# A chunked delta-rule recurrence with a channel mix: inputs w and a in a tile apart from b and k with earlier loads, a readout in four array pieces and two banks, and a mix in 768-column instructions

## The chip, the cores and the metric

One core of one Trainium2 chip runs the whole kernel. The metric is the device time of one execution, in microseconds (us); lower is better.

## The reference

Six arrays r, k, v, w, a, b of shape 4 batches x 8 heads x 768 steps x 40 go through a recurrence over the steps with a 40x40 state per head; what it reads out goes through a channel mix with three weight matrices.

```python
for t in range(S):
    y[:, :, t] = einsum('bhd,bhde->bhe', r[t], state)
    Sa = einsum('bhde,bhe->bhd', state, a[t])
    state = state * w[t][:, :, None, :] - outer(Sa, b[t]) + outer(v[t], k[t])
x = y as (batch, step, 320); x_prev = x one step earlier
xk = mu_k * x + (1 - mu_k) * x_prev;  xr likewise with mu_r
out = sigmoid(xr @ w_r) * (relu(xk @ w_k) ** 2 @ w_v)      # 320x320, 320x1024, 1024x320
```

All is float32. The two inputs of a matrix product of the channel mix are split into a high and a low part, and three partial products are added.

## The kernel before

**Tiling.** The 768 steps are cut into 12 chunks `k` of 64 (`C`). The 32 heads are handled in two parts `p` of 16; within a part two heads are stacked on the partitions (rows 0 to 39 and 64 to 103, `ROWS`; `EP` = 104) and eight such pairs lie side by side (`G` = 8). Inside a chunk the recurrence is turned into small matrix products and one triangular solve.

**The steps of a chunk.** `front` (four pieces on the vector engine, DVE: a running product of w, a reverse scan, w times a into `az`, and the decay times b and k) and the scores `psc` and transposes `pkt` run two chunks ahead of the chunk that uses them. Before a front, `check` has the scalar engine (ACT) test that w lies in range; it reads the first part of the loaded tile. The triangular solve `tri` is a recurrence of 30 steps on GpSimd (POOL), two chunks ahead as well: `tri_out` writes the 32x32 blocks of the scores to DRAM, `tri` reads them back in another layout and solves, `tri_store` writes the result to DRAM, `tri_back` reads it into `sn`. The chain of the chunk itself has five stages, z, T, L, U, s: 64 small matmuls each (lines 413, 419, 425, 431, 437), and after each a copy on ACT (`zs`, `vu`) that the next stage needs. T and the stages behind it read the solved `sn`. Then come `put`, `pgh`, the readout `py` (lines 499 and 504) and the product with the decay on DVE (`xp`). `send_x` moves `xp` by DMA into `x` in the layout of the channel mix; `Mix` does the channel mix of that chunk during the next two chunks, one piece at a time.

**What sets the order.** Everything is recorded in the order in which it is written (`manual_schedule`), and each engine works its own instructions off in that order, DMA issues on the queue of SyncE (SP) included. `STEP` is a hand-written list of 25 slots, numbered 0 to 24, that every chunk goes through; a word is a step and its part (`w0`: load for part 0). `M` is one piece of Mix (or, at first, of the conversion of the weights), `F` one piece of a front. `later(n, ...)` puts an instruction off to the end of the n-th slot from here.

```python
STEP = [x.split() for x in (
    "z0 z1 F", "M F r0", "T0 T1 F", "M pmt0 q1 r1", "L0 L1 F", "M pmt1 F", "U0 U1 F", "M psc0 F", "s0 s1", "M psc1", "M put0 to",
    "M put1 v", "M pgh0", "M tl", "py0", "M pgh1 ts", "M pkt0", "M py1", "pkt1 tk", "M w0 x", "M w1", "M", "M",
    "M Q0", "M F")]
AHEAD = dict(r=(0, load_rv), w=(3, load_wab), Q=(3, check), q=(2, check), psc=(2, scores), pkt=(2, pkt))
```

So `w0` in slot 19 of chunk k loads all of w, a, b and k of chunk k+3, part 0, as one tile `wab`, and `Q0` in slot 23 has ACT read it. `wab` has two buffers; the one that is filled was read last by `pkt0` in slot 16. `w1` and `q1` (slot 3 of the next chunk) are the same for part 1. Before slot 0 of chunk 0 a prologue loads and prepares chunks 0, 1 and part of 2.

**Banks.** The tag `sw` has three PSUM banks, taken in turn by `psc` (2 each), `put` (2), `pgh` (2), `py` (1), `pkt` (2) and `pmt` (1): whoever takes one waits until what was written there three takes earlier has been read out.

## Time and profile before

| what | value |
|---|---|
| times of three runs | 703.68, 711.09, 702.17 us |
| the profiled execution: span from its first to its last instruction | 707.3 us |
| its own time | not given beside the span; the span lies among the three times |
| busy: PE, DVE, ACT, POOL | 541.4, 440.4, 313.9, 396.5 us |
| mean granted TensorE clock | 0.843 |
| moved by DMA | 71.15 MB, mean 101 GB/s |
| stages by the starts of line 413: prologue; chunk 0; 1; 2; 3 to 9 together; 10; 11 and the rest | 76.8; 56.7; 82.8; 44.1; 343.4; 33.9; 69.6 us |

PE is the matmul engine, PEld its weight loads. "Lnnn" is a line of the kernel. In the timeline a row is: start, duration, engine, line, operation, out<-in, count, and in brackets the idle time ahead of it and what ended that. In the views of waits a row is: who waited, for whom, total us, how often, the longest.

### The profile page before, as it was taken

What the parts mean: (1) busy time and instruction counts of PE and PEld (TensorE: products, weight loads), DVE (VectorE), ACT (ScalarE), POOL (GpSimd) and SP (SyncE); (2) the same over time, 40 slices, a digit from 0 to 9 for tenths busy, and PEclk for the clock granted to TensorE, in tenths of its full rate; (3) what the DMA queues carried; (4) which work ended last, traced back from release to release, by engine and by line L of the source; (5) the groups of instructions that cost most, each with busy time, mean ns of one, the idle gap of its engine ahead of it and who ended that gap; (6) DMA issues with size and microseconds to landing.
All of it is one profiled execution on the core that took longest, in us unless ns stands there. A gap on an engine that the chain in (4) does not pass through costs nothing. (4 is left out here: it accounts for less than half of the span.)

```text
span 707.3 us, 24797 instructions
## 1 busy us (share of the span) xinstructions
PE 541.4 (77%) x10658; PEld 496.2 (70%) x10658; DVE 440.4 (62%) x773; ACT 313.9 (44%) x793; POOL 396.5 (56%) x814
## 2 busy tenths in 40 slices
PE   1103256605498999989989979899799799999994
PEld 1103245505398888979878979889798799999984
DVE  6577558629846828738648468287386476463551
ACT  2112142114346546445545445464455445656562
POOL 4286683860078369388388585792882883830000
PEclk9999996555578895895988968958959859999998
DMA  5532757482245264463583563644635706332100
GB/s 139 115 92 43 181 111 136 118 189 62 48 100 132 68 131 105 102 128 70 115 159 67 115 140 70 130 103 102 128 71 114 167 21 128 86 79 67 45 25 23
DMA packets 120555, 71.15 MB, mean 101 GB/s; under 512 B 96574, under 2 KB 110870, under 8 KB 118150
## 3 DMA queue, kind: packets, MB, share of 16 engines
q1 hardware_dynamic: 118214, 63.74, 42.6%
q10 hardware_dynamic: 2223, 5.76, 3.1%
q8 instruction: 85, 1.39, 0.8%
q14 instruction: 33, 0.26, 0.1%
HBM read 52.98 MB, written 10.22 MB: 89 GB/s over the span
## 5 line engine op out<-in xcount | busy, mean ns | idle before, releaser
L387 POOL TENSOR_TENSOR td<-td,ttmp 128x30 f32<-128x30 f32 (+4 forms) x360 | 175.3, 487 | 28.2
L384 POOL TENSOR_TENSOR ttmp<-ta,td 128x30 f32<-128x30 f32 (+4 forms) x360 | 174.1, 484 | 28.3
L112 PE MATMUL ph<-xk,wkh 120*128 120x256 f32 x480 | 99.6, 306 | 6.2 <-ACT xk L90 5.2
L378 POOL TENSOR_SCALAR_AFFINE_SELECT td<-ta 64x512 f32<-64x512 f32 x24 | 18.4, 765 | 139.2 <-DMA ta<-tx 138.1
L90 DVE TENSOR_TENSOR hl<-hf,hh 128x256 fp32r<-128x256 f32 x96 | 43.2, 450 | 64.4 <-ACT hh L90 63.7
L112 PEld LDWEIGHTS ph<-xk,wkh 120*128 120x128 f32 x480 | 75.5, 200 | 10.8 <-ACT xk L90 5.7
L333 PE MATMUL psc<-az,wab 40*64 40x64 f32 x1536 | 39.4, 275 | 54.0 <-DVE wab L318 43.2
L333 PEld LDWEIGHTS psc<-az,wab 40*64 40x64 f32 x1536 | 35.6, 184 | 58.8 <-issue 55.7
L306 DVE TENSOR_TENSOR_SCAN pe<-wab,first 104x520 f32<-104x520 f32 x24 | 31.1, 1296 | 67.5 <-ACT pe L90 46.7
L90 ACT ACTIVATE hf<-ph 128x256 f32<-128x256 f32 x96 | 36.6, 381 | 75.8 <-PE ph L112 75.5
L112 PE MATMUL pv<-wvh,hh 128*128 128x320 f32 x192 | 68.8, 358 | 1.8 <-issue 1.8
L419 PE MATMUL ch<-zs,sn 32*32 32x40 f32 x768 | 21.9, 229 | 62.6 <-ACT zs L90 62.6
L112 PE MATMUL ph<-xk,wkl 120*128 120x256 f32 x288 | 68.2, 292 | 0.0
L419 PEld LDWEIGHTS ch<-zs,sn 32*32 32x32 f32 x768 | 20.1, 134 | 65.3 <-ACT zs L90 64.7
L112 PE MATMUL pv<-wvh,hl 128*128 128x320 f32 x192 | 61.6, 321 | 0.0
L112 PE MATMUL pv<-wvl,hh 128*128 128x320 f32 x192 | 61.3, 319 | 0.0
L90 POOL TENSOR_TENSOR mc<-zs,pe 104x320 f32<-104x320 f32 x24 | 17.9, 767 | 58.7 <-DVE zs L90 58.0
L112 PEld LDWEIGHTS ph<-xk,wkl 120*128 120x128 f32 x288 | 50.7, 201 | 0.0
L90 DVE TENSOR_TENSOR az<-psc,mask 64x512 f32<-64x512 f32 x48 | 33.1, 689 | 22.3 <-PE psc L333 21.5
L90 ACT COPY vu<-ch 32x320 f32<-32x320 f32 x96 | 40.0, 416 | 12.9 <-PE ch L419 11.3
L112 PEld LDWEIGHTS pv<-wvh,hh 128*128 128x128 f32 x192 | 37.7, 197 | 6.0 <-issue 2.1
L90 ACT ACTIVATE hf<-hf 128x256 f32<-128x256 f32 x96 | 40.0, 417 | 3.1
(95 smaller groups left out, 1213.2 us busy)
## 6 DMA issues: line engine op xcount, KB each, us to landing
wab<-in_wab_dram SPq DMA_DIRECT2D x22, 835.7 KB
vr<-in_rvd_dram SPq DMA_DIRECT2D x24, 416.0 KB
ta<-tx SPq DMA_DIRECT2D x24, 256.0 KB
vu<-in_vt_dram SPq DMA_DIRECT2D x24, 256.0 KB
out_dram<-sig SPq DMA_DIRECT2D x48, 80.0 KB
tx<-sn SPq DMA_DIRECT2D x48, 64.0 KB
ty<-td SPq DMA_DIRECT2D x24, 128.0 KB
sn<-ty SPq DMA_DIRECT2D x48, 64.0 KB
```

The costliest lines, as they stand in the source:

```text
L90: f(*args, **kw)
L112: nc.tensor.matmul(out, lhsT=left[i][g], rhs=right[j][g], start=start and k == 0, stop=stop and k == len(terms) - 1)
L306: nc.vector.tensor_tensor_scan(out=pe.rearrange("p x t -> p (x t)"), data0=w[:, 0:SP], data1=first, initial=0.0, op0=ALU.mult, op1=ALU.add)
L333: nc.tensor.matmul(to[64 * y:64 * y + 64, x], lhsT=kb[r0:r1, x, y], rhs=az[r0:r1, i, x], start=True, stop=True)
L378: nc.gpsimd.affine_select(out=TD[h], in_=TA[h, i::2], compare_op=ALU.is_gt, fill=0.0, base=-i, pattern=[[-2, 16], [1, 32]], channel_multip ...
L384: nc.gpsimd.tensor_tensor(out=tmp, in0=TA[:, s:s + 1, s + 1:].broadcast_to([128, rows, n]), in1=TD[:, 0:rows, s:s + 1].broadcast_to([128, ...
L387: nc.gpsimd.tensor_tensor(out=TD[:, 0:rows, s + 1:], in0=TD[:, 0:rows, s + 1:], in1=tmp, op=ALU.subtract)
L419: mm(c3[a:a + 32, x], lhsT=sn[a:a + 32, x, 0:32], rhs=zs[a:a + 32, x], start=True, stop=True)
```

## The change

The input `wab` becomes two: `wa` (w and a, 104x1033) and `kb` (b and k, 104x1024), each in tiles of its own with two buffers. `wa` of chunk k+3 is loaded in slots 3 and 8 of chunk k, `kb` in slots 18 and 20. In the readout the state's transposed copy `mk` is one dense 104x104 block per pair, not four padded ones, so that the first half of `py` runs on 40-row pieces, and the two heads of a pair go to two banks, each with its own `xp`. In the mix, the difference, the high and the low part are one instruction of 768 columns each in place of three of 256, and the mix has five pieces in place of seven. In the start-up the order of the constants on POOL changes, and mu_k and mu_r are loaded behind the first inputs and weights.

```diff
-    "z0 z1 F", "M F r0", "T0 T1 F", "M pmt0 q1 r1", "L0 L1 F", "M pmt1 F", "U0 U1 F", "M psc0 F", "s0 s1", "M psc1", "M put0 to",
-    "M put1 v", "M pgh0", "M tl", "py0", "M pgh1 ts", "M pkt0", "M py1", "pkt1 tk", "M w0 x", "M w1", "M", "M",
+    "z0 z1 F", "M F r0", "T0 T1 F", "M pmt0 q1 r1 a0", "L0 L1 F", "M pmt1 F", "U0 U1 F", "M psc0 F", "s0 s1 a1", "M psc1",
+    "M put0 to", "M put1 v", "M pgh0", "M tl", "py0", "M pgh1 ts", "M pkt0", "M py1", "pkt1 tk b0", "M x", "M b1", "M", "M",
     "M Q0", "M F")]
...
-                for g in range(3):
-                    nc.vector.tensor_tensor(out=d4[:, g], in0=x[:, g, :, 1:], in1=x[:, g, :, 0:C], op=ALU.subtract)
+                nc.vector.tensor_tensor(out=diff.rearrange("p g b t -> p (g b) t", b=NB),
+                                        in0=by_b[:, :, 1:], in1=by_b[:, :, 0:C], op=ALU.subtract)
                 yield
...
-                    for g in (2, 0, 1):
-                        xm = moe.tile([128, TT4], F32, tag="xm", name="xm", bufs=2)[:NP] if nm == "k" else diff[:, g]
+                    xm = moe.tile([NP, 3, TT4], F32, name="xm") if nm == "k" else diff
+                    for g in range(3):
                         nc.vector.scalar_tensor_tensor(
...
-                        later(0, nc.scalar.copy, hi[:, g], xm)
-                        later(1, nc.vector.tensor_tensor, out=lo[:, g], in0=xm, in1=hi[:, g].bitcast(F32), op=ALU.subtract)
-                        if g == 2:
-                            later(2, nc.sync.dma_start, lo[80:120, 2].bitcast(F32), hi[40:80, 2].bitcast(F32))
-                        yield
+                        if g == 1:
+                            yield
+                    later(0, nc.scalar.copy, hi, xm)
+                    later(1, nc.vector.tensor_tensor, out=lo, in0=xm, in1=hi.bitcast(F32), op=ALU.subtract)
+                    later(2, nc.sync.dma_start, lo[80:120, 2].bitcast(F32), hi[40:80, 2].bitcast(F32))
+                    yield
...
-            def load_wab(k, p, parts=((0, WP + 3 * G * C),)):
+            def load_wa(k, p, parts=((0, WP + G * C),)):
+                x = att.tile([EP, WP + G * C], F32, tag="wa", name=f"wa_{k}_{p}", bufs=2)
...
+            def load_kb(k, p):
+                x = st[k, p]["kb"] = att.tile([EP, G, 2, C], F32, tag="kb", name=f"kb_{k}_{p}", bufs=2)
+                nc.sync.dma_start(x, kb[k, p])
...
-                for q, (r0, r1) in enumerate(ROWS):
-                    later(0, nc.scalar.copy, mk[r0:r1, :, :, q, 0:HD], p4[r0:r1, :, :, 0:HD])
+                later(0, nc.scalar.copy, mk, pt[0:EP].rearrange("d (x e) -> d x e", x=4)[:, :, 0:EP])
...
-                y = ps("sw", f"py_{k}_{p}").rearrange("e (x t) -> e x t", t=C)
+                ys = [ps("sw", f"py_{k}_{p}_{q}").rearrange("e (x t) -> e x t", t=C) for q in range(2)]
...
-                            nc.tensor.matmul(y[r0:r0 + n, 2 * x + q], lhsT=mk[:, x, i, q, 0:n], rhs=r[:, x, i],
+                            nc.tensor.matmul(ys[q][r0:r0 + n, x], lhsT=mk[d0:d1, x, r0:r0 + n], rhs=r[d0:d1, x, i],
...
-                for x in range(4):
-                    for q in range(2):
+                for q in range(2):
+                    for x in range(4):
...
+                for q in range(2):
+                    later(0, nc.vector.tensor_tensor, out=xp[:, q], in0=ys[q][0:EP, 0:4].rearrange("e (b j) t -> e b j t", b=2),
...
-            AHEAD = dict(r=(0, load_rv), w=(3, load_wab), Q=(3, check), q=(2, check), psc=(2, scores), pkt=(2, pkt))
+            AHEAD = dict(r=(0, load_rv), a=(3, load_wa), b=(3, load_kb), Q=(3, check), q=(2, check), psc=(2, scores), pkt=(2, pkt))
```

On SP's queue, from `tk` (the read-back into `sn`, slot 18) of one chunk to the scores' way out (`tx<-sn`, slot 10) of the next, this stands before (x is the channel mix's input, vr the tile of v and r):

```order
L371 DMA sn_4004<-ty 32x16x32 x4
L277 DMA wab_0_5360<-in_wab_dram 104x2057
L521 DMA x_5362<-xp_5187 40x12x64 x2
L523 DMA x_5362<-xp_5187 40x4x64 x3
L277 DMA wab_1_5381<-in_wab_dram 104x2057
L400 DMA vr_0_5484<-in_rvd_dram 104x4x256
L400 DMA vr_1_5544<-in_rvd_dram 104x4x256
L90 DMA xk<-xk 40x256
L362 DMA tx<-sn_5660 32x16x32 x4
```

And this of the changed kernel at the same place:

```order
L377 DMA sn_3174<-ty 32x16x32 x4
L284 DMA kb_0_4515<-in_kb_dram 104x1024
L526 DMA x_4526<-xp_4351 40x12x64 x2
L528 DMA x_4526<-xp_4351 40x4x64 x3
L284 DMA kb_1_4545<-in_kb_dram 104x1024
L406 DMA vr_0_4646<-in_rvd_dram 104x4x256
L406 DMA vr_1_4707<-in_rvd_dram 104x4x256
L279 DMA wa_0_4709<-in_wa_dram 104x1033
L85 DMA xk<-xk 40x256
L279 DMA wa_1_4890<-in_wa_dram 104x1033
L368 DMA tx<-sn_4818 32x16x32 x4
```

The half with w and a, which `check` reads, has moved behind vr and is now that of the chunk after: it is issued a chunk earlier relative to its use. The half with b and k stands where `wab` stood.

On DVE, from the `hl` of slot 13 (the low part of the mix's hidden layer) to the masked scores of `pgh1` in slot 15 (`gh_1`), this stands before:

```order
L90 TENSOR_TENSOR hl<-hf,hh 128x256
L90 TENSOR_TENSOR xr<-diff,xr 120x256
L90 TENSOR_TENSOR hl<-hf,hh 128x256
L90 TENSOR_TENSOR xr<-diff,xr 120x256
L90 TENSOR_TENSOR xp_6843<-py_0_6810,pe_0_4586 104x2x4x64
L147 SCALAR_TENSOR_TENSOR diff<-diff,mur,x_6190 120x256
L90 TENSOR_TENSOR gh_1_0_6861<-pgh_1_0_6863,mask 128x512
L90 TENSOR_TENSOR gh_1_1_6862<-pgh_1_1_6864,mask 128x512
```

And this of the changed kernel:

```order
L85 TENSOR_TENSOR hl<-hf,hh 128x256 x2
L85 TENSOR_TENSOR xr<-diff,xr 120x768
L85 TENSOR_TENSOR xp_6817<-py_0_0_6783,pe_0_4578 104x2x2x64
L85 TENSOR_TENSOR xp_6817<-py_0_1_6784,pe_0_4578 104x2x2x64
L85 TENSOR_TENSOR gh_1_0_6834<-pgh_1_0_6836,mask 128x512
L85 TENSOR_TENSOR gh_1_1_6835<-pgh_1_1_6837,mask 128x512
```

All of the low part of xr now stands ahead of `xp`, in one instruction, and `xp` is two instructions, one for each bank; `pgh1` takes the bank that the first of them frees.

## The prediction

> **What bounds the kernel now.** The page comes first: its slices show where the span goes.

> ```profile
> PE   1103256605498999989989979899799799999994
> PEclk9999996555578895895988968958959859999998
> ```

> From slice 12 on PE is busy nearly all the time, yet the granted clock falls to about half once in every chunk. A busy PE is then a slow PE. So the stages come next, cut at the starts of the chain (line 413); the columns are start:end and length, the busy us of PE, PEld, DVE, ACT and POOL, the granted clock, DMA's share and GB/s:

> ```profile
> 216.30:260.40 44.10, 42.26 (x891) 38.55 (x890) 30.89 (x54) 25.25 (x64) 26.57 (x51) 0.88 0.47 104
> 260.40:310.10 49.70, 46.66 (x889) 42.92 (x888) 31.23 (x54) 24.52 (x63) 33.25 (x67) 0.79 0.52 104
> ...
> 553.50:603.80 50.30, 46.65 (x890) 42.87 (x889) 31.89 (x57) 24.48 (x63) 34.00 (x69) 0.80 0.48 104
> 603.80:637.70 33.90, 33.90 (x729) 31.44 (x728) 18.90 (x38) 20.15 (x53) 18.91 (x46) 1.00 0.36 82
> 216.30:637.70 421.40, 394.31 (x7833) 361.55 (x7832) 269.57 (x465) 216.78 (x558) 279.06 (x558) 0.84 0.50 105
> ```

> Chunks 3 to 9 take 49.1 us each (603.8 - 260.4, by 7) at a clock of 0.79 to 0.89. Chunk 10, which has no chunk 12 to prepare, takes 33.9 at 1.00. One of the slow chunks, number 6, cut in three:

> ```profile
> 405.40:412.50 7.10, 3.14 (x73) 2.83 (x72) 1.46 (x3) 2.31 (x7) 6.08 (x13) 1.00 0.86 172
> 412.50:430.60 18.10, 18.06 (x351) 16.62 (x351) 15.81 (x23) 10.07 (x25) 16.32 (x23) 0.53 0.40 88
> 430.60:454.60 24.00, 24.00 (x472) 21.95 (x470) 14.14 (x29) 12.10 (x32) 11.86 (x33) 1.00 0.56 114
> ```

> PE stands still for 4 us early on, then works for 18.1 us at 0.53, then at full clock. Who stops it, by the waits of PE, ACT and POOL over chunks 3 to 9 (who, for whom: us, times, longest), and the timeline at that place:

> ```profile
> PE ch L419 <- ACT zs L90: 24.0, 7, 4.0
> ACT pe L90 <- DMA wab<-in_wab_dram: 28.2, 6, 5.2
> POOL td L378 <- DMA ta<-tx: 74.8, 12, 11.7
> 402.78 0.40 SPq L277 DMA_DIRECT2D wab<-in_wab_dram  x1
> 410.13 0.72 ACT L90 ACTIVATE pe<-wab,limit 104x512 f32<-104x512 f32 x1 [5.20 <-DMA wab<-in_wab_dram]
> 412.00 0.74 ACT L90 COPY zs<-ch 128x320 f32<-128x320 f32 x2
> 412.48 1.60 PE L419 MATMUL ch<-zs,sn 32*32 32x40 f32 x64 [3.96 <-ACT zs L90]
> ```

> The 836 KB load is issued at 402.78 and lands some 7 us later. ACT works in order: `check` (pe) waits for the load, and `zs`, which stage T needs, stands behind it. All seven chunks show it: 24.0 us, 3.4 each. The lost clock costs more: at 0.53, 18.1 us do the work of 9.6, 8.5 us lost.

> **The change, part by part.** *The load of w and a* now goes out in slots 3 and 8 for a use in slot 23 and in slot 3 of the next chunk, more than 20 us ahead where 7 sufficed for twice the bytes. Its buffer is free once the front two chunks ahead has run, before it is issued; what queues behind it on SP (xk, the scores' way out) needs the same fronts anyway. So ACT's wait goes: 3.4 us, and the half-clock stretch behind it with it. b and k arrive for slots 2 and 7, nine slots after slot 18: hidden, while SP isn't late.

> *The readout.* Line 499 runs 32 instructions on whole rows; `pgh` (line 483) already has the 40-row pieces that it will have:

> ```profile
> 439.28 1.15 PE L499 MATMUL py<-vr,mk 104*64 104x64 f32 x32
> 440.21 1.11 PE L504 MATMUL py<-gh,kt 128*40 128x64 f32 x32
> 442.39 1.16 PE L483 MATMUL pgh<-vr 40*64 40x64 f32 x64
> 443.48 0.42 PE L112 MATMUL pv<-wvh,hh 128*128 128x320 f32 x1
> ```

> From start to start 32 take 0.93 us, and pgh's 64 take 1.09; 32 such take 0.55. Two readouts a chunk save 0.8 us of PE.

> *The mix and the second bank.* Widths that exist give the price of 768 columns:

> ```profile
> L139 DVE TENSOR_TENSOR diff<-x 120x256 f32<-120x256 f32 x36 | 19.1, 580 | 0.0
> L90 DVE TENSOR_TENSOR gh<-pgh,mask 128x512 f32<-128x512 f32 x48 | 30.9, 685 | 15.3 <-PE pgh L483 15.3
> L318 DVE TENSOR_TENSOR wab<-wab 104x1024 f32<-104x1024 f32 x24 | 31.5, 1312 | 0.4
> L90 ACT CAST xr<-diff 120x256 fp32r<-120x256 f32 x36 | 14.5, 402 | 1.2 <-DVE diff L147 1.2
> L90 ACT COPY sn<-psc 128x512 f32<-128x512 f32 x24 | 14.1, 586 | 39.0 <-PE psc L333 39.0
> ```

> On DVE 768 lies half-way between 685 and 1312 ns, 1.0 us; on ACT 402 and 586 ns continue to 0.77. A chunk's `diff` goes from 1.74 to 1.0 us, each low part from about 1.4 to 1.0, and the two halves of `xp` cost 0.27 more per part: about 1 us less of DVE's 31 per chunk. ACT saves about 1.6 of 24.5 (mixes 0.9, `mk` in one copy 0.7). Neither bounds a chunk, so I count nothing. But `pgh1` now takes a bank that the first `xp` must empty, and all of xr's low part stands ahead of `xp`:

> ```profile
> 440.25 0.41 ACT L90 CAST hh<-hf 128x256 fp32r<-128x256 f32 x1
> ```

> Chunk 6: hh ends at 440.66, xr's high part at 441.4, its low part at 442.4, the first `xp` (about 0.5, 256 columns) at 442.9; pgh1, due at 442.39 - 0.4 = 442.0, would wait 0.9 us. Its bounds are 0 (DVE gets there earlier) and 1.8 (as much again, with ACT and DVE late by one instruction each); I take 0.9. Behind it on PE stands all the rest of the chunk.

> *The fronts on DVE.* In the first two stretches of chunk 6 DVE is busy for 1.5 + 15.8 = 17.3 us, where PE without stall and throttle needs 3.1 + 9.6 = 12.7. The fronts must end before the second scores, due at about 14 (12.7 and one more piece of mix, 1.3). Of the 17.3, some 2 isn't front and stands behind, and the mix saves 0.5 here: 14.8, so a wait of 0.8. Its bounds are 0 (fronts that start ahead of slot 0) and 17.3 - 12.7 = 4.6; I take 1.0.

> *PE's floor.* Without stall and throttle chunk 6 takes 3.1 + 9.6 + 24.0 = 36.7 us; less 0.8, plus 0.9 and 1.0: **37.8**.

> *What is late next: POOL.* The solve, the two `mc` behind it, the wait, and the last solve, beside which no front runs:

> ```profile
> 433.60:435.10 1.50, 1.50 (x16) 1.24 (x16) 1.46 (x3) 0.71 (x3) 1.43 (x2) 1.00 0.23 34
> 435.10:444.40 9.30, 9.30 (x234) 8.37 (x232) 7.92 (x18) 5.29 (x15) 0.00 (x0) 1.00 0.76 178
> 444.40:481.60 37.20, 34.00 (x576) 31.69 (x574) 21.64 (x34) 17.62 (x45) 31.85 (x64) 0.73 0.49 97
> 593.60:624.20 30.60, 30.60 (x632) 28.16 (x632) 14.59 (x30) 18.88 (x50) 25.00 (x64) 1.00 0.39 86
> 433.18 0.59 ACT L90 COPY sn<-psc 128x512 f32<-128x512 f32 x1 [0.71 <-PE psc L333]
> 442.80 1.28 SPq L367 DMA_DIRECT2D ty<-td  x2
> 448.38 2.90 SPq L371 DMA_DIRECT2D sn<-ty  x4
> ```

> POOL needs 37.2 + 1.5 = 38.7 us a chunk and idles 9.3, most of which a 37.8 us chunk no longer has. The DVE work that lay in these 9.3 us (7.9 busy) then lies beside a solve. The bounds: it stretches nothing (38.7), or each of its microseconds blocks POOL (46.6). The two solves are nearest: 7.0 us more of DVE cost 6.6, but that was the fronts, which ran beside the solve already. For the rest I take 1.3: POOL's pace is **40.0 us**.

> When that bites: the scores leave PE at 433.2, 27.8 into chunk 6 and 15.3 without stall and throttle; `ta` lands 11.2 later, the solve takes 37, the way back into `sn` 8.5 (442.80 to 451.28) and a landing of about 2 (an estimate): 74 us into a chunk, where T two chunks on comes at 2 x 37.8 + 3 = 78.6. A lead of 4.6, lost at 2.2 a chunk (and 0.9 less at the first): chunks 2 to 6 go at PE's floor, 7 to 9 at 40.0, and chunk 10, which waits for the last solve, takes some 37. What PE then waits for is `sn` at T and, since x stands behind `tk` on SP, a late x on DVE.

> [...]

> *The start-up.* Two small loads no longer stand ahead of the first one, and `check` of chunk 2 waits for half the bytes:

> ```profile
> 0.83 0.48 SPq L102 DMA_DIRECT2D muk<-in_mu_k_dram  x1
> 1.36 0.34 SPq L102 DMA_DIRECT2D mur<-in_mu_r_dram  x1
> 95.70 0.72 ACT L90 ACTIVATE pe<-wab,limit 104x512 f32<-104x512 f32 x1 [7.18 <-DMA wab<-in_wab_dram]
> 159.10 2.34 PE L419 MATMUL ch<-zs,sn 32*32 32x40 f32 x64 [23.53 <-ACT zs L90]
> ```

> 0.8 for the first, 2 for the second (bounds 0 and 3.6, half of the wait). In chunk 1 ACT keeps T waiting for 23.5 us, behind weight loads among which the chunk-3 inputs come too; half of these now go earlier: 3 us (bounds -2 and 10). Together 6.

> *The sum*, for the profiled execution: 5 x 37.8 + 3 x 40.0 + 37 = 346 us, where the row says 421.4: 75.4 less. With the start-up 81.4. The last 69.6 us (PE-bound from the start of chunk 11) stay. 707.3 - 81.4 = 625.9; the profiled execution lies 3.6 us above the median of 703.7, so **622 us** for the median.

> **The rivals.** *The clock stays low.* Chunk 2 had no wait at T, and yet:

> ```profile
> 225.95 0.63 PE L112 MATMUL pv<-wvh,hh 128*128 128x320 f32 x1 [1.84 <-issue]
> ```

> After 1.84 us of standstill the clock was halved and the chunk took 44.1. If each of the smaller waits left (0.9 at pgh1, 1.0 at the scores, up to 2 for `sn`) does this, chunks take 44.1 - 0.8 = 43.3: 8 of them and chunk 10 with 34 make 380, 41 less; with the start-up **657**. Against it: a halved chunk is slower than POOL, which then regains its lead, so that the next ones don't wait; the mean falls back to POOL's pace. [...]

> *POOL keeps up* (its lower bound or better): 8 x 37.8 + 34 = 336, 85 less; with the start-up **613**. It needs a solve near 35 us; those beside fronts took 37.

> *DVE blocks POOL fully*, the upper bound of POOL's pace: 2 x 37.8 + 6 x 46.6 + 37 = 392, 29 less: **668**. For it the two solves, against it the 14.6 us of DVE beside the last, unstretched one.

> *The change doesn't do what it says*, since DMA is the limit: then b and k come late at slot 2 and DVE, then PE, waits as long as now. For it: the 7 us landing, and 0.86 DMA share at 172 GB/s ahead of the stall. Against it: a mean share near 0.5. Only the start-up and the readout are left, 6 and 8 x 0.8: **691**.

> *Slower: the second bank.* If pgh1's wait reaches the 1.84 us of chunk 2, the clock is halved in the dense second half as well; 17 us at half cost 8.5. With a first halving in place (43.3) and the longer wait a chunk takes 43.3 + 1.8 + 8.5 = 53.6, 4.5 more than now: 8 x 4.5 - 6: **734**. It decides at a wait of some 1.8 us, twice what I find.

> **How the numbers follow.** Forecast 0.50 (own range 612 to 642), clock 0.25, POOL keeps up 0.11, DVE blocks POOL 0.04, wait not removed 0.06, second bank 0.04. The range goes from 604, where POOL keeps up and the two new waits are half of what I took, to 664, which leaves out the last three and a part of the clock's case. A measurement of this kernel tells 2% from no change: below 689.6 is faster. The first four are, 0.90; the wait not removed is mostly within 2%, 0.06; slower 0.04.

> **What the new profile would show.** ACT's wait of `pe` for a DMA gone from chunk 2 on; no 3 us gap ahead of line 419's stage, or one whose `sn` is late; POOL without its 9 us wait for `ta`, solves of 37 to 39 us end to end; chunks of 38, then 40 us; a clock near 1.0 in the chunks; a gap below 1 us at pgh1, released by `xp`. Wrong I would be if the clock is halved again in each chunk, if POOL still idles while PE waits, or if DVE waits for b and k.

## The result, and the profile after

The changed kernel takes 634.5 us (median of four runs, 627.5 to 636.4) where the kernel before takes 703.5 in the same rounds: a ratio of 0.902, 95% interval 0.895 to 0.908. The forecast was 622 with a range of 604 to 664: the sign and the main mechanism were right, the size was 12 us too good. The profiled execution has a span of 634.4 us.

The page's slices of TensorE's busy share and of its granted clock, after the change:

```profile
PE   2204238534569999999899999999999899999995
PEclk9999998555558789999999999999999999999999
```

The clock no longer falls once per chunk: from slice 15 on (238 us) it stays at nine tenths or more. The same by stages, cut at the starts of stage z (chunks 2, 3, 6, 9, 10, and 11 with the rest; the columns are as in the prediction):

```profile
206.10:249.90 43.80, 42.19 (x889) 38.17 (x888) 30.48 (x50) 24.28 (x59) 26.41 (x49) 0.88 0.49 112
249.90:289.70 39.80, 38.04 (x889) 34.38 (x888) 31.23 (x50) 22.98 (x58) 34.97 (x66) 1.00 0.59 134
370.00:410.40 40.40, 38.23 (x891) 34.39 (x890) 31.63 (x50) 23.07 (x58) 35.49 (x67) 1.00 0.57 133
490.30:531.50 41.20, 38.22 (x889) 34.43 (x888) 32.00 (x52) 22.54 (x57) 36.14 (x69) 1.00 0.47 103
531.50:565.90 34.40, 33.83 (x729) 30.95 (x728) 17.96 (x34) 19.06 (x47) 20.76 (x47) 1.00 0.38 82
565.90:634.40 68.50, 58.84 (x907) 54.76 (x906) 27.70 (x58) 34.22 (x83) 1.44 (x2) 0.98 0.16 37
```

Chunks 3 to 9 take 281.6 us, 40.2 each, where they took 343.4, 49.1 each: 62 of the 73 us that the span lost. All seven stand at clock 1.00 in this execution. The start-up (to the start of chunk 2) went from 216.3 to 206.1. Chunk 2 alone is still halved and takes 43.8. What TensorE waits for in chunks 3 to 9 now:

```profile
PE py L503 <- DVE gh L85: 3.9, 7, 0.6
PE ch L443 <- ACT vu L85: 3.3, 5, 1.0
PE ch L437 <- issue: 2.3, 3, 0.9
PE psc L339 <- DVE kb L324: 2.3, 5, 0.8
PE pgh L487 <- DVE xp L85: 1.6, 7, 0.3
PE ch L443 <- issue: 0.8, 1, 0.8
PE psc L339 <- issue: 0.3, 1, 0.3
```

Stage T's 24 us are gone from the list, and ACT has no wait of `pe` for a DMA in this stretch. The rows add up to 14.5 us, 2.1 per chunk; with 38.2 us busy that is the 40.2. GpSimd, which idled 9.3 us ahead of each solve, now goes from one solve into the next (end of a solve, the two `mc`, start of the next one):

```profile
278.66 0.30 POOL L397 MEMSET td<- 64x16 f32 x2
279.04 1.44 POOL L85 TENSOR_TENSOR mc<-zs,pe 104x320 f32<-104x320 f32 x2
280.43 1.69 POOL L384 TENSOR_SCALAR_AFFINE_SELECT td<-ta 64x512 f32<-64x512 f32 x2
...
319.29 1.44 POOL L85 TENSOR_TENSOR mc<-zs,pe 104x320 f32<-104x320 f32 x2
```

From `mc` to `mc` are 40.25 us without a pause: as long as TensorE's chunk. So two readings of the 40.2 stood open: TensorE with its small waits, or GpSimd's pace, as the prediction had it. What each part of the change brings stood open too.

### The profile page after: what moved, and what is told of

It is laid out like the page before. It is cut to its first block, busy times and chain, and to the rows that moved or that the text cites. A ratio compares the mean times of both kernels' runs of the same rounds, so it can differ in the third digit from the quotient of the medians.

```text
span 634.4 us, 24776 instructions
## 1 busy us (share of the span) xinstructions
PE 492.3 (78%) x10658; PEld 446.0 (70%) x10658; DVE 440.2 (69%) x725; ACT 297.5 (47%) x721; POOL 414.4 (65%) x812
## 3 DMA queue, kind: packets, MB, share of 16 engines
q1 hardware_dynamic: 121022, 63.74, 44.7%
## 4 chain that ended last, share of the span: by engine, by line
PE 39%; DVE 28%; POOL 11%; DMA 9%; issue 6%; ACT 3%; SPq 2%; ACTq 0%; DVEq 0%; POOLq 0%
PE pv L103 9%; PE ph L103 9%; POOL td L393 5%; POOL ttmp L390 5%; DVE az L85 3%; DVE kb L324 3%; DMA wa<-in_wa_dram 3%; PE pgh L487 3%; PE pr L103 3%; DVE vu L85 2%; DVE pe L311 2%; PE py L508 2%; DVE az L321 2%; DMA x<-xp 2%; PE ch L419 2%
## 5 line engine op out<-in xcount | busy, mean ns | idle before, releaser
L390 POOL TENSOR_TENSOR ttmp<-ta,td 128x30 f32<-128x30 f32 (+4 forms) x360 | 188.5, 524 | 28.3
L393 POOL TENSOR_TENSOR td<-td,ttmp 128x30 f32<-128x30 f32 (+4 forms) x360 | 179.8, 499 | 28.2
L103 PE MATMUL ph<-xk,wkh 120*128 120x256 f32 x480 | 95.6, 297 | 5.3 <-ACT xk L85 4.3
L103 PEld LDWEIGHTS ph<-xk,wkh 120*128 120x128 f32 x480 | 72.2, 192 | 9.5 <-ACT xk L85 4.5
L339 PE MATMUL psc<-az,kb 40*64 40x64 f32 x1536 | 34.9, 252 | 53.5 <-DVE kb L324 53.2
L339 PEld LDWEIGHTS psc<-az,kb 40*64 40x64 f32 x1536 | 31.3, 163 | 57.4 <-issue 48.8
L103 PE MATMUL pv<-wvh,hh 128*128 128x320 f32 x192 | 65.9, 343 | 1.3 <-issue 1.3
L85 DVE TENSOR_TENSOR gh<-pgh,mask 128x512 f32<-128x512 f32 x48 | 30.8, 682 | 17.8 <-PE pgh L487 17.8
L85 DVE TENSOR_TENSOR az<-psc,mask 64x512 f32<-64x512 f32 x48 | 33.1, 689 | 11.2 <-PE psc L339 10.3
L85 ACT CAST hh<-hf 128x256 fp32r<-128x256 f32 x96 | 39.0, 406 | 3.0
L311 DVE TENSOR_TENSOR_SCAN pe<-wa,first 104x520 f32<-104x520 f32 x24 | 31.8, 1327 | 11.2 <-ACT pe L85 11.1
```

The costliest lines, as they stand in the source:

```text
L85: f(*args, **kw)
L103: nc.tensor.matmul(out, lhsT=left[i][g], rhs=right[j][g], start=start and k == 0, stop=stop and k == len(terms) - 1)
L311: nc.vector.tensor_tensor_scan(out=pe.rearrange("p x t -> p (x t)"), data0=w[:, 0:SP], data1=first, initial=0.0, op0=ALU.mult, op1=ALU.add)
L339: nc.tensor.matmul(to[64 * y:64 * y + 64, x], lhsT=kb[r0:r1, x, y], rhs=az[r0:r1, i, x], start=True, stop=True)
L390: nc.gpsimd.tensor_tensor(out=tmp, in0=TA[:, s:s + 1, s + 1:].broadcast_to([128, rows, n]), in1=TD[:, 0:rows, s:s + 1].broadcast_to([128, ...
L393: nc.gpsimd.tensor_tensor(out=TD[:, 0:rows, s + 1:], in0=TD[:, 0:rows, s + 1:], in1=tmp, op=ALU.subtract)
```

## The experiments

### Which part brought the gain

Three kernels: the loads alone, everything but the loads, and everything but the mix. (Loads and mix without the readout were not run.) First the loads alone, on the kernel before:

```diff
-    "z0 z1 F", "M F r0", "T0 T1 F", "M pmt0 q1 r1", "L0 L1 F", "M pmt1 F", "U0 U1 F", "M psc0 F", "s0 s1", "M psc1", "M put0 to",
-    "M put1 v", "M pgh0", "M tl", "py0", "M pgh1 ts", "M pkt0", "M py1", "pkt1 tk", "M w0 x", "M w1", "M", "M",
+    "z0 z1 F", "M F r0", "T0 T1 F", "M pmt0 q1 r1 a0", "L0 L1 F", "M pmt1 F", "U0 U1 F", "M psc0 F", "s0 s1 a1", "M psc1",
+    "M put0 to", "M put1 v", "M pgh0", "M tl", "py0", "M pgh1 ts", "M pkt0", "M py1", "pkt1 tk b0", "M x", "M b1", "M", "M",
...
-            def load_wab(k, p, parts=((0, WP + 3 * G * C),)):
+            def load_wa(k, p, parts=((0, WP + G * C),)):
...
+            def load_kb(k, p):
...
```

> The kernel before with one part of the change: w and a apart from b and k, and the new slots for their loads. The readout, the mix and the order of the start-up stay as before. Theory A (the gain is ACT's wait for the load and the half clock behind it; the readout and the mix lie off the path): chunks 3 to 9 go at 40 to 41 us as in the changed kernel, no stretch at half clock in them, total 634 to 645 us. Rival (the gain is shared: shorter readout, shorter ACT and DVE work are needed for the stall to go): chunks of 43 to 46, total 655 to 690.

Measured: 655.3 us, ratio 0.936 (0.928 to 0.944); chunks 3 to 9 at 44.0. The rival's numbers came true, by another mechanism: the loads alone do take the wait at T away, but each chunk has a new one at stage U (here line 435), and a halved clock behind it. The waits of TensorE in the loop, and the timeline of ACT and TensorE in chunk 7:

```profile
PE ch L435 <- ACT zs L90: 18.0, 7, 2.6
430.69 0.40 ACT L90 CAST xk<-xm 120x256 fp32r<-120x256 f32 x1 [1.80 <-DVE xm L147]
431.00 0.85 ACT L90 COPY mk<-pmt 40x320 f32<-40x320 f32 x2
431.87 0.72 ACT L90 ACTIVATE pe<-wa,limit 104x512 f32<-104x512 f32 x1
432.71 0.75 ACT L90 COPY zs<-ch 128x320 f32<-128x320 f32 x2
433.19 1.66 PE L435 MATMUL ch<-zs,sn 32*32 32x40 f32 x64 [2.58 <-ACT zs L90]
```

Again ACT stands in order behind something late, this time the mix: the first of the three high parts of xk waits 1.8 us for VectorE, which is busy with the front, and `mk`, `pe` and `zs` stand behind it. The kernel before has the same wait on ACT; there TensorE, at half clock behind the stall at T, was still busy when `zs` came, and stage U (line 431) began without a wait. Chunk 6 of the kernel before:

```profile
419.18 0.40 ACT L90 CAST xk<-xm 120x256 fp32r<-120x256 f32 x1 [1.79 <-DVE xm L147]
421.68 2.34 PE L431 MATMUL ch<-zs,sn 32*32 32x40 f32 x64
```

The reverse, the changed kernel with `wab` whole and loaded in slots 19 and 20:

```diff
-    "z0 z1 F", "M F r0", "T0 T1 F", "M pmt0 q1 r1 a0", "L0 L1 F", "M pmt1 F", "U0 U1 F", "M psc0 F", "s0 s1 a1", "M psc1",
-    "M put0 to", "M put1 v", "M pgh0", "M tl", "py0", "M pgh1 ts", "M pkt0", "M py1", "pkt1 tk b0", "M x", "M b1", "M", "M",
+    "z0 z1 F", "M F r0", "T0 T1 F", "M pmt0 q1 r1", "L0 L1 F", "M pmt1 F", "U0 U1 F", "M psc0 F", "s0 s1", "M psc1", "M put0 to",
+    "M put1 v", "M pgh0", "M tl", "py0", "M pgh1 ts", "M pkt0", "M py1", "pkt1 tk", "M w0 x", "M w1", "M", "M",
...
```

> The changed kernel with the loads as before: w, a, b and k in one tile, loaded in slots 19 and 20. Theory A: ACT's wait and the half clock stay, chunks 3 to 9 at about 48 us (49.1 less 0.8 of readout), total 692 to 703. Rival (the shorter readout and mix move the instructions of ACT so that the stall shrinks): chunks of 45 or less, total under 685.

Measured: 688.3 us, ratio 0.983 (0.974 to 0.992); chunks 3 to 9 at 46.6, between the two expectations. The stall stays, somewhat shorter (before: 24.0 us, longest 4.0). It halves the clock in five of the seven chunks; in chunks 7 and 8 a standstill of 1.9 and 2.0 us does so that the profile puts down to "issue" (the last section):

```profile
PE ch L421 <- ACT zs L85: 14.7, 7, 3.3
```

Then the changed kernel with the mix of before:

```diff
-                    for g in range(3):
+                    for g in (2, 0, 1):
...
-                        if g == 1:
-                            yield
-                    later(0, nc.scalar.copy, hi, xm)
...
+                        later(0, nc.scalar.copy, hi[:, g], xm)
...
+                        yield
...
```

> The changed kernel with the mix in 256-column instructions as before; loads and readout stay changed. In the kernel with the loads alone ACT waits 1.8 us for the first xm ahead of mk and zs, and TensorE 2.6 us for zs at the third part of the chain, with the clock halved behind it. Theory M (it is the mix that took this wait away, since one high-part copy comes after zs where three small ones stood ahead of it): the wait stays at 2 to 2.6 us and halves the clock, chunks 3 to 9 at 43 to 44, total 648 to 656. Rival R (it is the readout, whose one copy of mk is 0.35 us shorter on ACT, and 0.8 us less on TensorE): the wait falls below 1.3 us, chunks at 40 to 41, total 634 to 642.

Measured: 652.1 us, ratio 0.926 (0.919 to 0.933); chunks at 43.2. Theory M is right: the wait and the halved clock stay without the new mix. TensorE's waits and ACT in this kernel, and then ACT and TensorE's stage s (line 443) at the same place in the changed one:

```profile
PE ch L435 <- ACT zs L85: 15.2, 7, 2.9
342.01 0.40 ACT L85 CAST xk<-xm 120x256 fp32r<-120x256 f32 x1 [2.26 <-DVE xm L138]
343.44 0.74 ACT L85 COPY zs<-ch 128x320 f32<-128x320 f32 x2
```

```profile
337.54 0.74 ACT L85 COPY zs<-ch 128x320 f32<-128x320 f32 x2
340.83 0.83 ACT L85 CAST xk<-xm 120x768 fp32r<-120x768 f32 x1 [2.56 <-DVE xm L139]
342.08 1.71 ACT L85 COPY vu<-ch 32x320 f32<-32x320 f32 x4
342.98 1.68 PE L443 MATMUL ch<-vu,kt 128*40 128x40 f32 x64 [1.01 <-ACT vu L85]
```

With one high part of 768 columns, recorded behind the third `xm`, ACT still waits (2.56 us), but now behind `zs`. The next copy that the chain needs, `vu`, now stands behind that wait, and stage s waits for it for 1.0 us at most, in five of the seven chunks: too little to halve the clock here. So, by these rows, the mix's gain isn't its shorter instructions; it is that a wait changed places with a copy that the chain needs. No kernel changed the place alone. In steps: loads 6.4%, the readout with the new start-up 1.0% more, the mix 2.4% more; the middle step isn't clear of the noise, since the intervals of the two ratios overlap. Loads times the rest alone (0.936 x 0.983) would give 0.920; the changed kernel has 0.902. Each part needs the other, since either stall alone is enough to halve the clock.

### Early, or half of the bytes

```diff
-    "z0 z1 F", "M F r0", "T0 T1 F", "M pmt0 q1 r1 a0", "L0 L1 F", "M pmt1 F", "U0 U1 F", "M psc0 F", "s0 s1 a1", "M psc1",
-    "M put0 to", "M put1 v", "M pgh0", "M tl", "py0", "M pgh1 ts", "M pkt0", "M py1", "pkt1 tk b0", "M x", "M b1", "M", "M",
+    "z0 z1 F", "M F r0", "T0 T1 F", "M pmt0 q1 r1", "L0 L1 F", "M pmt1 F", "U0 U1 F", "M psc0 F", "s0 s1", "M psc1",
+    "M put0 to", "M put1 v", "M pgh0", "M tl", "py0", "M pgh1 ts", "M pkt0", "M py1", "pkt1 tk", "M a0 b0 x", "M a1 b1", "M", "M",
```

> The changed kernel with w and a in their own tile, but loaded late: in slots 19 and 20 where the kernel before loads, b and k right behind. Is it the earliness or the half of the bytes? Where the earliness is needed: ACT waits 2 us or more for w and a in slot 23, PE at stage T for 1.5 to 3 us, the clock is halved behind it, chunks of 44 to 48, total 660 to 695. Where half of the bytes is enough: the load lands about when ACT is there, PE waits under 1 us at T, the clock stays at 1.0, chunks at 40 to 41, total 632 to 642.

Measured: 656.4 us (652.4 to 662.4), ratio 0.936 (0.926 to 0.945); chunks at 43.5 in the profiled execution, the longest of the four, with a span of 660.7. Neither expectation fits as a whole. Its waits in the loop, and the wait ahead of the 3.1 us (chunk 4):

```profile
PE ch L437 <- issue: 6.8, 4, 2.4
ACT pe L85 <- DMA wa<-in_wa_dram: 5.9, 5, 1.9
PE ch L443 <- ACT vu L85: 3.1, 1, 3.1
PE ch L437 <- ACT zs L85: 2.5, 3, 1.5
306.62 0.83 ACT L85 CAST xk<-xm 120x768 fp32r<-120x768 f32 x1 [4.53 <-DVE xm L139]
```

Half of the bytes shorten ACT's wait to 1.9 us at most, and T waits only once, for 0.7 us; but single standstills of 1.5 to 3.1 us are left, and the clock is halved in six of seven chunks. Only one of the six stands behind a wait of ACT for the load. One stands behind ACT's wait for VectorE ahead of `vu`, and four behind standstills that the profile puts down to "issue" (1.7 to 2.4 us, in two of the four with a shorter wait for `zs` beside it), which the last section takes up. Beside the other parts the late loads give 4.7% (0.983 to 0.936), the early ones 8.1% (to 0.902). So the split alone brings more than half. That earliness brings the rest fits the four times, but by which way the late load costs it is not shown.

### Does GpSimd set the pace of 40.2?

The two `mc` on VectorE:

```diff
-                later(0, nc.gpsimd.tensor_tensor, out=mc[:, :, 0:HD], in0=zs[0:EP], in1=decay, op=ALU.mult)
+                later(0, nc.vector.tensor_tensor, out=mc[:, :, 0:HD], in0=zs[0:EP], in1=decay, op=ALU.mult)
```

> The changed kernel with the two products into mc (1.5 us a chunk) on VectorE in place of GpSimd. Theory A (GpSimd, back to back at 38.9 + 1.5 = 40.4 us, sets the pace of chunks 3 to 9): chunks fall to about 39, 7 x 1.4 = 10 us less, total 622 to 628. Rival B (TensorE sets it, 38.2 us busy and 1.8 of small waits for DVE and ACT; GpSimd is merely as long): chunks stay at 40 or grow with DVE's 1 us more, total 633 to 642.

Measured: 642.3 us, ratio 0.917 (0.908 to 0.925): no gain. The reason is place: `mc` stands ahead of the first `gh` on VectorE, and the readout, which needs the banks that `gh` empties, waits longer. Waits of TensorE, one of them, and two chunks, with and without a halved clock:

```profile
PE py L503 <- DVE gh L85: 9.3, 7, 1.5
394.50 0.68 PE L503 MATMUL py<-vr,mk 40*64 40x64 f32 x28 [1.52 <-DVE gh L85]
369.00:416.50 47.50, 45.03 (x891) 40.99 (x890) 32.02 (x52) 23.00 (x58) 40.74 (x80) 0.82 0.52 128
416.50:456.10 39.60, 38.06 (x891) 34.40 (x890) 30.74 (x51) 23.04 (x58) 27.32 (x51) 1.00 0.52 118
```

This is the mechanism of the rival "slower through the second bank", at another readout: a wait of 1.5 us, where the prediction saw its point at 1.8, was followed by a halved clock in four of the seven chunks, and the worst of them is 7.9 us longer than the chunk after it. Two tries to put `mc` (and then the gate's product too) behind `gh` with a longer delay followed:

```diff
-                later(0, nc.gpsimd.tensor_tensor, out=mc[:, :, 0:HD], in0=zs[0:EP], in1=decay, op=ALU.mult)
+                later(6 - p, nc.vector.tensor_tensor, out=mc[:, :, 0:HD], in0=zs[0:EP], in1=decay, op=ALU.mult)
```

> The changed kernel with the two mc products on VectorE, but in slot 16, behind the second gh, where VectorE waits for the readout, and not in slots 10 and 11, where they stood ahead of gh and made TensorE wait 1.5 us in py. If only that place made the earlier trial slow: py waits 0.6 us as in the changed kernel, no halving in chunks 3 to 9, chunks at 39.5 to 40, total 628 to 634. If GpSimd's pace of 40.4 us was what held the changed kernel: chunks at 38.5 to 39.2, total 622 to 628. If VectorE is the limit with 1 us more: chunks at 40.5 to 42, total 638 to 645.

```diff
-                    later(1, nc.vector.tensor_tensor, out=gates[q], in0=gates[q], in1=pv[q][:, :DM], op=ALU.mult)
+                    later(2, nc.vector.tensor_tensor, out=gates[q], in0=gates[q], in1=pv[q][:, :DM], op=ALU.mult)
...
```

> As the trial with mc on VectorE in slot 16, and the two products of gate and pv one slot later, so that they no longer stand ahead of gh on VectorE (0.9 us), for which the readout waits 0.6 us a chunk. If TensorE's waits set the pace: another 0.5 us a chunk less than the trial with mc alone, chunks at 39 to 39.4, total 624 to 630. If something else sets it: no difference to that trial.

Measured: 641.6 and 639.5 us (ratios 0.914 and 0.910), as the first. Neither edit did what it says: `mix_rest` empties the whole queue of `later`, and in the trace `mc` and the gate's product still stand ahead of `gh`. They say nothing on GpSimd. So `mc` got a step of its own in slot 16, and the changed kernel ran beside it:

```diff
-    "M put0 to", "M put1 v", "M pgh0", "M tl", "py0", "M pgh1 ts", "M pkt0", "M py1", "pkt1 tk b0", "M x", "M b1", "M", "M",
+    "M put0 to", "M put1 v", "M pgh0", "M tl", "py0", "M pgh1 ts", "M pkt0 mc0 mc1", "M py1", "pkt1 tk b0", "M x", "M b1", "M", "M",
...
```

> The changed kernel itself once more, beside the next three on the same chip: chunks 3 to 9 at 39.8 to 40.4 us with no halved clock, total 630 to 638, so that the trial with mc behind gh can be compared with it directly.

> The changed kernel with the two mc products on VectorE, each in a step of its own behind the second gh and ahead of the second xp (in the earlier trial they still ran ahead of the first gh, because the mix empties the queue of what is put off). If the earlier trials were slow only by their place: py waits 0.6 us or less, no stretch at half clock in chunks 3 to 9, chunks at 39.2 to 39.8, total 626 to 632. If GpSimd's work mattered to the pace by its length, the same. If VectorE has no room for 0.9 us more: some other small wait of TensorE grows by as much, chunks at 40 or more, total 634 to 642.

Measured on the same chip: the changed kernel 632.3 us (0.902, 0.892 to 0.912), with `mc` in slot 16 629.8 (0.899, 0.891 to 0.908): no difference that can be measured. Against both expectations, some chunks are at a halved clock: chunks 7 and 8 of the changed kernel (41.3 and 44.7 us) and 3, 7 and 8 of the other (42.2, 44.3 and 40.7). Chunk 2 of the changed kernel, on the other hand, is not halved this time (40.2). The same kernel thus has halvings at other places in another execution. With `mc` in slot 16, GpSimd's waits over the loop, and chunk 5, one without a halving:

```profile
POOL td L384 <- DMA ta<-tx: 14.9, 13, 5.9
324.20:364.40 40.20, 38.11 (x891) 34.41 (x890) 32.41 (x52) 23.01 (x58) 33.95 (x65) 1.00 0.59 132
```

GpSimd now has time to wait for its input, and the chunks without a halving are as long as ever. Its pace wasn't the bound, though it was as long. Last, a solve with a fifth of its steps left out:

```diff
                 for s in range(1, 31):
+                    if 13 <= s < 19:
+                        continue
```

> The changed kernel with steps 13 to 18 of the 30 of each solve left out (its output is not the reference's): GpSimd needs some 10 us less per chunk. If GpSimd sets the pace: chunks 3 to 9 fall to about 38.2 to 38.8 us. If TensorE's own work and its small waits for VectorE and ACT set it (38.2 + 1.8): chunks stay at 39.5 to 40.

Measured: 630.6 us, in one run. Clocks are halved in chunks 3, 7 and 8. Three chunks without (4, 5 and 6), and what TensorE waits for in the second of them:

```profile
282.80:321.90 39.10, 38.09 (x891) 34.39 (x890) 30.24 (x50) 23.03 (x58) 28.48 (x51) 1.00 0.54 126
321.90:361.10 39.20, 38.10 (x891) 34.41 (x890) 30.25 (x50) 23.06 (x58) 30.32 (x56) 1.00 0.61 134
361.10:401.50 40.40, 38.39 (x890) 34.44 (x889) 30.89 (x50) 23.02 (x58) 29.80 (x55) 1.00 0.62 136
PE ch L445 <- ACT vu L85: 0.6, 1, 0.6
PE psc L339 <- DVE kb L324: 0.2, 1, 0.2
```

The first two fit neither expectation: 39.1, not 38.5 and not 40. The third stands still for 1.5 us that the profile puts down to "issue". VectorE's busy time falls from between 31.2 and 31.6 in these chunks of the changed kernel to between 30.2 and 30.9, with the same 50 instructions. In chunks 4 and 5 TensorE's waits fall from 1.8 and 2.2 us to 0.9 and 0.8, and the chunks from 39.9 and 40.4 to 39.1 and 39.2: their length follows TensorE's waits. These rows suggest that GpSimd costs about 1 us a chunk here, by slowing VectorE and not by being late; it is one execution of one kernel.

### What halves the clock

Copies on ACT that nobody needs, ahead of the first `zs`; two as shown here, four in the second kernel:

```diff
...
+                if p == 0 and k > 2:
+                    for _ in range(2):
+                        later(0, nc.scalar.copy, spare, wvspare)
                 later(0, nc.scalar.copy, zs, c3)
```

> The changed kernel with two copies of 128x512 between buffers that nothing else uses, on ACT ahead of the first zs of each chunk from chunk 3 on: zs comes 1.17 us later, TensorE has 0.4 us to spare there, so it should stand still for 0.8 us at stage T. [...] Rival (any wait at this place lets the clock fall): chunks of 44 or more.

> The same with four copies: zs 2.35 us later, a standstill of some 1.9 us at T. [...]

Measured, in one run each: with two 630.0 us and 40.2 per chunk, no clock halved. But no wait of T (line 431 in these kernels) is listed either, so the standstill that was to be tried never came about, and this kernel says nothing on the clock. With four 644.6 us and 41.4: T waits 1.14 us in each of the seven chunks, not 1.9, so the spare time there had been taken too small (1.2, not 0.4). The clock was halved in one chunk of seven. Two stretches of 3.41 us with that wait, chunks 4 and 5, and the wait in the second:

```profile
290.00:293.41 3.41, 2.27 (x70) 1.96 (x68) 3.02 (x4) 2.78 (x7) 3.17 (x4) 1.00 0.62 166
330.95:334.37 3.42, 2.29 (x72) 1.97 (x71) 2.98 (x4) 2.81 (x7) 3.18 (x4) 1.00 0.74 187
332.86 1.34 PE L431 MATMUL ch<-zs,sn 32*32 32x40 f32 x64 [1.14 <-ACT zs L85]
```

TensorE was busy 2.27 of 3.41 us in the first, and the clock stayed; 2.29 in the second, and it was halved for 17.1 us. At one and the same busy share, 0.67, the clock thus did both; the last section has the count over all traces.

## Why the prediction was right, and where it was off

**The load's wait and the half clock behind it: right**, with a gap. The wait at T went. That the clock would then stay up rested on no other wait being there; the next one, at stage U, was overlooked, though ACT's wait of 1.79 us stood in the trace before. The *mix*, for which the prediction counted nothing, took it away: 43.2 us a chunk without it, 40.2 with it. That the mix was part of the change was luck, as far as the forecast goes.

**The work at half clock: mis-sized, and the main error.** The prediction took the 18.1 us at 0.53 as 9.6 us of work. Chunk 6 of the changed kernel, cut at the same places (351 matmuls in the middle piece in both):

```profile
370.00:373.07 3.07, 3.07 (x71) 2.83 (x70) 2.75 (x4) 2.11 (x7) 2.83 (x4) 1.00 0.81 124
373.07:384.96 11.89, 10.95 (x351) 9.87 (x350) 11.22 (x16) 8.31 (x20) 11.03 (x12) 1.00 0.56 144
384.96:410.40 25.44, 24.21 (x474) 21.70 (x470) 17.67 (x32) 12.65 (x32) 21.63 (x53) 1.00 0.55 128
```

The same work takes 10.95 us at full clock, 1.65 times less, not 1.88 times: 7.1 us were lost and not 8.5. The clock's share isn't the share of the time, since these matmuls don't take twice as long at half clock: from start to start the 64 of stage L took 2.28 us halved (chunk 6 before) and 1.26 at full clock (chunk 6 after), the six of `pv` behind them 1.77 and 1.00.

**The readout:** line 499 was busy 16.0 us in 14 readouts, line 503 is 11.8: 0.6 us a chunk, 0.8 predicted. **The new waits, at the second bank and at the fronts:** predicted 0.9 at `pgh` and 1.0 at the scores. The second bank costs 1.6 + 3.9 us in seven chunks, 0.8 each, but mostly one readout earlier than thought, at `py` waiting for `gh`; the scores cost 0.3; `vu` (0.5) and standstills that the profile puts down to "issue" (0.5) had not been seen. Together 2.1 for 1.9.

**PE's floor** was thus 40.2 and not 37.8. Of the 2.4 us, 1.4 come from the half clock and 0.2 each from the readout and the waits. The remaining 0.6 or so lie in the last third of the chunk, where TensorE is busy for 24.2 us and 24.0 less the readout's saving had been expected; why is open. **GpSimd's pace** was foreseen at 40.0 and measured at 40.25, but it isn't what bounds the chunks. The forecast of 40 for chunks 7 to 9 was right for a wrong reason; since TensorE was no faster than GpSimd, the lead was never used up, and chunk 10 didn't wait for the last solve (34.4, where 37 was forecast). The prediction's upper bound of 46.6, by which each microsecond of VectorE blocks GpSimd, was not reached: the solve and its `mc` took 40.25. The landing in `sn`, an estimate of about 2 us there, took 1.6 in the trace before (the last issue ended at 451.27, the last update of its semaphore came at 452.85).

**The start-up:** 10.2 us in place of 6, most of it in chunk 1 (82.8 to 76.7). **Chunk 2** was forecast at the floor and is halved in the profiled execution.

The sum of the misses, in the profiled executions: start-up -4.2, chunk 2 +6.0, chunks 3 to 6 +9.3 (160.5 for 151.2), 7 to 9 +1.1, chunk 10 -2.6, the rest -1.1: +8.5, which is 634.4 for 625.9. Part of that closeness is luck: misses of opposite sign cancel, and the pace of chunks 7 to 9 was right without its reason. Of the rivals, "the clock stays low" had the mechanism right: the clock was halved behind waits of 1.14 us (four copies, in one chunk of seven), 1.5 us (`mc` on VectorE) and 1.84 us (chunk 2 before). It failed on size, since the waits left in chunks 3 to 9 are 1.0 us at most.

## What to carry to other kernels

An engine that works in order hands every wait on to what stands behind it, as ACT did here (with the loads alone, `xk` waited 1.80 us for VectorE, and stage U 2.58 us for `zs` behind it); when one such wait is removed, look for the next instruction of that queue that waits ahead of a copy which the critical chain needs, and move it behind, and then look at what has come to stand behind it there. In these traces the price of a standstill of 1.5 to 3 us is its length and, mostly more, what is lost at half clock behind it: 1.4 to 8.5 us, an estimate from the 3.4 to 20.5 us that a halving lasts here and the 7.1 lost in 17.1. So the aim here is no standstill above 1 us: behind 1329 stretches with less the clock was never halved. Take the time of halved work from the same instructions at full clock in another chunk, not from the clock's share, and don't take an engine that is busy all the time for the bound until something has been taken from it.

## What the runs showed of the hardware

```
below 0.56       42    42
0.56 to 0.71     42    17
above 0.71     1329     0
```

So, in these traces, the clock was halved behind every stretch with a standstill of 1.5 us and more (a share below 0.56: 42 of 42), behind 17 of 42 with one of 1.0 to 1.5 us, and behind none of the 1329 with a shorter one. What decides between the two outcomes in the middle row is not shown.

**The larger standstills that the profile puts down to "issue" end at one distance from the start of an instruction transfer.** One of the larger ones, in chunk 8 of the changed kernel's second run, and the row of the queue that is spoken of below:

```profile
452.76 0.48 PE L437 MATMUL ch<-zs,sn 32*32 32x40 f32 x16
454.95 1.61 PE L437 MATMUL ch<-zs,sn 32*32 32x40 f32 x48 [1.71 <-issue]
...
q8 instruction: 85, 1.39, 1.0%
```

TensorE stops in the middle of 64 equal matmuls, and the profile shows nothing that they wait for. The page's third part shows a queue of 85 instruction transfers of 16 KB; the trace has their starts. The end of the standstill, its length, the start of the last such transfer, and the difference:

```
changed kernel, chunk 2     215.21   1.32   212.45   2.76
changed kernel, second run  454.95   1.71   452.20   2.75
before, chunk 2             225.95   1.84   223.30   2.65
mc in slot 16               415.12   1.84   412.35   2.77
late loads                  393.17   2.41   390.71   2.46
```

All 35 standstills of 0.7 us and more that the 14 traces put down to "issue" between 205 and 560 us end 2.46 to 2.98 us after such a start. By chance about one in twelve would (an estimate from this span of 0.52 us and the 814 transfers in 14 times 355 us, one every 6.1 us); on the other hand, only 35 of the 814 transfers are followed by such a standstill. The standstill of 1.84 us in chunk 2, on which the prediction leaned, is one of them. Such standstills also stand ahead of four of the six halvings in the chunks 3 to 9 of the late loads, and of the longest ones in the second run of the changed kernel and with `mc` in slot 16. It is a pattern in the traces; no run tested it by changing the number of instructions, and why a standstill follows at these places and not behind the other transfers stays open.
